# Expert slots of 448, 384 and 256 tokens for the experts' rests, in a fused retention, expert and feed-forward kernel

## Chip, cores and metric

One core of one Trainium2 chip. The metric is the device time of one execution, in microseconds (us); lower is better. Three runs of the kernel before have a median of 1375.33 us.

## What is computed

Three steps over 4608 tokens of 512 features, all in float32 (cut from the reference):

```python
# 1. retention: 8 batches, 8 heads, 576 positions, 64 features a head
ret = scale * (q @ k.T) * Dmat           # Dmat: causal, gamma_h ** (i - j)
x = (ret @ v) as (4608, 512)
# 2. experts: each token goes to one of 8
logits = x @ w_gate + modality_bias[modality_id]
e_idx = argmax(logits, axis=1)
gate_w = softmax(logits)[e_idx]
for e in range(8):
    mask = e_idx == e
    h = maximum(x[mask] @ w1[e], 0.0)    # 512 -> 1024
    out[mask] = gate_w[mask] * (h @ w2[e])   # 1024 -> 512
# 3. feed-forward
h = maximum(out @ w_in, 0.0)             # 512 -> 2048
return (h * h) @ w_out                   # 2048 -> 512
```

How many tokens an expert gets is known only when the kernel has computed the logits.

## The kernel before

**Stages.** `phase0` computes the retention and the routing, tile by tile of 128 tokens. `phase12` runs the experts. `phase3` runs the feed-forward, with an order of instructions that a planner (`Plan`) makes from a list of costs; the change doesn't touch it. The order of the other two is written out by hand.

**Slots.** Tokens of one expert are gathered into a slot and computed together. There are ten slots: `"E"`, of 512 tokens, takes the first 512 of the expert that leads after 32 of the 36 tiles, so that work can begin before the routing is done; slots 0 to 7 are 512 wide and slot 8 (`NF`) is 256 wide. Behind them stand seven guarded slots (`extra`, `NX`), which run only if the count `slots[:, 3]` says so: one branch, passed by all engines at unit 73, skips them together. A guarded slot goes over its weights twice, for two output columns at a time, with one buffer of each kind.

**Units.** A slot is eight units (`us`, index i), one for each 128 of the 1024 inner features. In unit i TensorE runs `first` of unit i+1 (12 matmuls: 4 blocks of 128 features, each in three terms of high and low parts) and then `second` of unit i (12 more, into four banks). The moving operand is as wide as the slot (`width`). ScalarE makes `hh` (the rectified product), VectorE `hl` (what is left over). Transposes of the next slot (`trans`, four of them per 128 features, one for each 128 tokens) stand between the two halves of units 3 to 6; ScalarE and VectorE split them into `xh` and `xl`. First products and transposes rotate through three banks.

**Beside it**, in the same hand-written order: weight loads (`wload`, three buffers `wr`), their split (`wsplit`, `wx` and `wy`, one per unit, four units ahead), the conversion of the float64 weights of the last stage (`convs`, dealt out at 2250 of its cost units per unit), and `combos`, which reads 512 finished columns (`eyr`) and makes the seven operands of the first block of `phase3`. SyncE issues nearly all transfers, in order; GpSimd issues the gathers (`gather`: a register load from `slots`, a copy of indices `ix`, one indirect transfer for each 128 tokens).

**The table.** `table` computes on VectorE, in 128 equal rows, what each slot holds: `slots[:, 0]` the expert, `slots[:, 1]` the first block in the token list, `slots[:, 2]` the output column at which it starts, `slots[:, 3]` the number of guarded slots. It is a generator: ten of its steps are taken in unit 1, between the steps of the last `route_b`; ten in unit 2; the rest in unit 3. Before, an expert's tokens fill consecutive slots, rounded up, and the expert whose last slot is emptiest comes last; if there are nine slots and that last piece is 256 or smaller, it goes into slot 8.

Of the kernel before, what the change touches and what calls it, by code (L numbers as in the profile page):

```python
# [9 lines left out]
F32 = mybir.dt.float32  # L10
# [15 lines left out]
P = 128  # L26
NTILE = NT // P
TS = 512
NF = 8
NX = 7  # L30
NS = NF + 1 + NX
KD = DM // P
LC = P + NE
DMAX = NTILE
# [10 lines left out]
def consts():  # L45
    gamma = 1.0 - 2.0 ** (-5.0 - np.arange(H, dtype=np.float64))
    scale = 1.0 / np.sqrt(float(D))
    tok = np.arange(9 * P)
    pos = (tok % S).astype(np.float64)
    vdec = scale * gamma[None, :] ** (-(pos[:, None] + 1.0))  # L50
    vdec = vdec.reshape(9, P, H).transpose(1, 0, 2)
    p = np.arange(S, dtype=np.float64)
    od = gamma[:, None] ** (p[None, :] + 1.0)
    od = od.reshape(KD, 2, 1, S)
    od[1::2] = od[1::2, ::-1].copy()
    odec = np.repeat(od, D, axis=2)
# [11 lines left out]
    rows["k512"] = 512.0 * np.arange(9)  # L68
    e = np.arange(NE)
    rows["le"] = (e[None, :] <= e[:, None]).astype(np.float64).reshape(-1)  # L70
    rows["eid"] = e
    rows["e36"] = DMAX * e
    s = np.arange(NS)
    rows["sv"] = np.where(s <= NF, s, s - 1)
# [17 lines left out]
def kernel(ctx, tc, qT, kT, kN, vN, modT, w_gate, mbias, w1, w2, w_in, w_out,  # L92
# [209 lines left out]
    def table():  # L302
        ps = count(NTILE, "psc")
        yield
        st = s1.tile([P, 4, NE], F32, tag="st", name="st")
        cm = s1.tile([P, NE, 9], F32, tag="cm", name="cm")
        rm = s1.tile([P, NE], F32, tag="rem", name="rem")
        mn = s1.tile([P, 1], F32, tag="mn", name="mn")
        isl = s1.tile([P, NE], F32, tag="isl", name="isl")
        nl = s1.tile([P, NE], F32, tag="nl", name="nl")  # L310
        le = s1.tile([P, NE, NE], F32, tag="le", name="le")
        en = s1.tile([P, NE], F32, tag="en", name="en")
        sn = s1.tile([P, NE], F32, tag="sn", name="sn")
        tot = s1.tile([P, 1], F32, tag="tot", name="tot")
        rl = s1.tile([P, 1], F32, tag="rl", name="rl")
        et = s1.tile([P, 1], F32, tag="et", name="et")
        mm = s1.tile([P, 2, NS, NE], F32, tag="mm", name="mm")
        ww = s1.tile([P, 4, NS, NE], F32, tag="ww", name="ww")
        rr = s1.tile([P, 4, NS], F32, tag="rr", name="rr")
        kk = s1.tile([P, NS], F32, tag="kk", name="kk")  # L320
        nsl, cnt = st[:, 0, :], st[:, 1, :]
        sv = row("sv")
        dve.scalar_tensor_tensor(out=cnt, in0=ise, scalar=-float(TS), in1=ps, op0=ALU.mult, op1=ALU.add)
        dve.tensor_copy(st[:, 2, :], row("eid"))
        dve.scalar_tensor_tensor(out=st[:, 3, :], in0=ise, scalar=4.0, in1=row("e36"), op0=ALU.mult,
                                 op1=ALU.add)
        yield
        dve.tensor_tensor(out=cm, in0=bc(cnt.unsqueeze(2), [P, NE, 9]),
                          in1=bc(row("k512").unsqueeze(1), [P, NE, 9]), op=ALU.is_gt)
        yield  # L330
        dve.tensor_reduce(out=nsl, in_=cm, axis=AX.X, op=ALU.add)
        yield
        dve.scalar_tensor_tensor(out=rm, in0=nsl, scalar=-float(TS), in1=cnt, op0=ALU.mult, op1=ALU.add)
        yield
        dve.tensor_reduce(out=mn, in_=rm, axis=AX.X, op=ALU.min)
        yield
        for _ in first_max(rm, mn, ALU.is_le, isl, "l"):
            yield
        dve.tensor_scalar(out=nl, in0=isl, scalar1=-1.0, scalar2=1.0, op0=ALU.mult, op1=ALU.add)
        yield  # L340
        dve.tensor_tensor(out=le, in0=row("le").rearrange("p (a b) -> p a b", a=NE),
                          in1=bc(nl.unsqueeze(1), [P, NE, NE]), op=ALU.mult)
        yield
        dve.tensor_tensor(out=le, in0=le, in1=bc(isl.unsqueeze(2), [P, NE, NE]), op=ALU.max)
        yield
        dve.tensor_tensor(out=le, in0=le, in1=bc(nsl.unsqueeze(1), [P, NE, NE]), op=ALU.mult)
        yield
        dve.tensor_reduce(out=en, in_=le, axis=AX.X, op=ALU.add)
        yield
        dve.tensor_tensor(out=sn, in0=en, in1=nsl, op=ALU.subtract)  # L350
        dve.tensor_tensor(out=mm[:, 0], in0=bc(en.unsqueeze(1), [P, NS, NE]),
                          in1=bc(sv.unsqueeze(2), [P, NS, NE]), op=ALU.is_le)
        dve.tensor_reduce(out=tot, in_=en, axis=AX.X, op=ALU.max)
        yield
        dve.tensor_tensor(out=mm[:, 1], in0=bc(sn.unsqueeze(1), [P, NS, NE]),
                          in1=bc(sv.unsqueeze(2), [P, NS, NE]), op=ALU.is_le)
        dve.tensor_tensor(out=ww[:, 0:2], in0=bc(mm[:, 0:1], [P, 2, NS, NE]),
                          in1=bc(st[:, 0:2, :].unsqueeze(2), [P, 2, NS, NE]), op=ALU.mult)
        dve.tensor_scalar(out=rl, in0=mn, scalar1=-256.0, scalar2=None, op0=ALU.is_le)
        yield  # L360
        dve.tensor_tensor(out=mm[:, 1], in0=mm[:, 1], in1=mm[:, 0], op=ALU.subtract)
        dve.scalar_tensor_tensor(out=rl, in0=tot, scalar=float(NF + 1), in1=rl, op0=ALU.is_equal,
                                 op1=ALU.mult)
        yield
        dve.tensor_tensor(out=ww[:, 2:4], in0=bc(mm[:, 1:2], [P, 2, NS, NE]),
                          in1=bc(st[:, 2:4, :].unsqueeze(2), [P, 2, NS, NE]), op=ALU.mult)
        yield
        dve.tensor_reduce(out=rr, in_=ww, axis=AX.X, op=ALU.add)
        yield
        dve.tensor_tensor(out=kk, in0=sv, in1=rr[:, 0, :], op=ALU.subtract)  # L370
        dve.tensor_copy(slots[:, 0, :], rr[:, 2, :])
        dve.tensor_scalar(out=tot, in0=tot, scalar1=-float(NF), scalar2=0.0, op0=ALU.add, op1=ALU.max)
        yield
        dve.tensor_scalar(out=kk, in0=kk, scalar1=8.0, scalar2=None, op0=ALU.min)
        dve.tensor_scalar(out=et, in0=rl, scalar1=-1.0, scalar2=1.0, op0=ALU.mult, op1=ALU.add)
        yield
        dve.scalar_tensor_tensor(out=slots[:, 1, :], in0=kk, scalar=4.0, in1=rr[:, 3, :], op0=ALU.mult,
                                 op1=ALU.add)
        dve.scalar_tensor_tensor(out=kk, in0=kk, scalar=float(TS), in1=rr[:, 1, :], op0=ALU.mult,
                                 op1=ALU.add)  # L380
        dve.tensor_tensor(out=tot, in0=tot, in1=et, op=ALU.mult)
        yield
        dve.tensor_scalar(out=kk, in0=kk, scalar1=float(TS), scalar2=float(NT), op0=ALU.add, op1=ALU.min)
        dve.tensor_scalar(out=et, in0=et, scalar1=float(NT), scalar2=None, op0=ALU.mult)
        dve.tensor_copy(slots[:, 3, :], bc(tot[:, 0:1], [P, NS]))
        yield
        dve.tensor_tensor(out=kk[:, NF:NF + 1], in0=kk[:, NF:NF + 1], in1=et, op=ALU.max)
        yield
        dve.tensor_copy(slots[:, 2, :], kk)
        yield  # L390

    def run(gen, n):
        for _ in range(n):
# [45 lines left out]
    X, XG = {}, {}  # L439

    def width(s):
        return 256 if s == NF else TS

    def gather(s):
        nt = width(s) // P
        rmax = (NTILE - G) * P if s == "E" else NT
        src = eslot[0:1, 1:2] if s == "E" else slots[0:1, 1, s:s + 1]
        reg = pool.value_load(src, min_val=0, max_val=KEYS - nt)
# [242 lines left out]
    def phase12():  # L691
        ring[0] = psG
        with ExitStack() as c1:
# [63 lines left out]
            def trans(s, c):  # L757
# [80 lines left out]
            def second(u, cols=range(KD)):  # L838
# [9 lines left out]
                if f == 7:  # L848
# [16 lines left out]
                    sp.dma_start(so.rearrange("(j p) -> j p", p=P), td[bass.ds(key, nt), :])  # L865

# [112 lines left out]
            for i, u in enumerate(us):  # L979
# [422 lines left out]
```

## Time and profile before

| | us |
|---|---|
| median of three runs | 1375.33 |
| lowest and highest | 1374.15, 1376.38 |
| the profiled execution | 1375.41 |
| its span, first to last instruction | 1373.6 |
| TensorE busy | 1334.8 |
| VectorE busy | 1022.4 |
| ScalarE busy | 627.4 |

The profile was taken in one execution; PE is TensorE, PEld its weight loads, DVE VectorE, ACT ScalarE, POOL GpSimd and SP SyncE. A matmul's recorded length includes its way through the array, so records overlap: the distance between starts is what one costs. "Idle before" is the time in which an engine stood still ahead of an instruction, with what ended it.

### The profile page before, as it was taken

To read this page: it belongs to the slowest core of one execution; us is meant where nothing else is said; L and a number is where in the kernel's file an instruction comes from. 1 tells how busy PE (TensorE), PEld (TensorE's weight loads), DVE (VectorE), ACT (ScalarE), POOL (GpSimd) and SP (SyncE) were. 2 spreads that over 40 slices of the span, in tenths; PEclk is the share of its full clock that TensorE was granted. 3 is DMA by queue.
4 is the path that set the end of the run, shared out by engine and by line. 5 is a ranking of instruction groups with operands and counts; after the bars stand their busy time and mean duration, and the time that the engine had idled before them with its cause. 6 is when DMAs were issued, how large, how long until landed. Compare 5 with 4: busy or idle time off the path is not lost.

```text
span 1373.6 us, 26947 instructions
## 1 busy us (share of the span) xinstructions
PE 1334.8 (97%) x10643; PEld 1228.3 (89%) x10643; DVE 1022.4 (74%) x2077; ACT 627.4 (46%) x1283; POOL 131.0 (10%) x170
## 2 busy tenths in 40 slices
PE   6999999999999999999999999999999999999997
PEld 5888877888888888879999999999999999999997
DVE  2787857878787787554888888867887777776765
ACT  1444444454445445444655555543344344443333
POOL 3222114101110110000000000000000011111121
PEclk9999999999999999999999999999999999999999
DMA  9988256778786886669545554577799756564451
GB/s 332 386 303 295 91 195 231 272 278 283 246 288 236 302 277 216 240 232 342 226 187 207 211 212 185 207 269 270 288 337 339 279 229 209 200 213 170 169 183 48
DMA packets 139380, 332.55 MB, mean 242 GB/s; under 512 B 15568, under 2 KB 50160, under 8 KB 139248
## 3 DMA queue, kind: packets, MB, share of 16 engines
q1 hardware_dynamic: 131120, 310.21, 63.1%
q0 software_dynamic: 5920, 19.40, 4.0%
q8 instruction: 84, 1.38, 0.4%
q10 hardware_dynamic: 2208, 1.17, 0.3%
q14 instruction: 48, 0.39, 0.1%
HBM read 222.59 MB, written 108.17 MB: 241 GB/s over the span
## 4 chain that ended last, share of the span: by engine, by line
PE 47%; DMA 3%; DVE 2%; ACT 0%; issue 0%; POOL 0%; SPq 0%; POOLq 0%
PE bank L1176 16%; PE bank L1174 16%; PE bank L1175 16%; DMA w<-wc 3%; DVE z L1152 1%; DVE h L1277 0%; DVE z L1160 0%; ACT h L1276 0%; POOL out L1284 0%; SPq L1047 0%; DVE oe L1152 0%; ACT z L1149 0%; DVE x L1152 0%; DVE yr L1152 0%; POOLq L1398 0%
## 5 line engine op out<-in xcount | busy, mean ns | idle before, releaser
L1174 PE MATMUL bank<-x,w 128*128 128x256 f32 x1008 | 285.9, 284 | 1.2 <-ACT z L1149 1.1
L1175 PE MATMUL bank<-w,h 128*128 128x256 f32 x1008 | 282.8, 281 | 3.7 <-DMA w<-wc 3.7
L1175 PE MATMUL bank<-x,w 128*128 128x256 f32 x1008 | 285.8, 284 | 0.5 <-DVE x L1152 0.5
L1174 PE MATMUL bank<-w,h 128*128 128x256 f32 x1008 | 282.7, 280 | 2.9 <-DVE oe L1152 1.6
L1176 PE MATMUL bank<-x,w 128*128 128x256 f32 x1008 | 285.0, 283 | 0.0
L1176 PE MATMUL bank<-w,h 128*128 128x256 f32 x1008 | 282.2, 280 | 0.7 <-DVE h L1277 0.7
L1149 ACT ACTIVATE z<-bank 128x256 f32<-128x256 f32 x288 | 108.7, 380 | 255.5 <-PE bank L1176 253.5
L1174 PEld LDWEIGHTS bank<-x,w 128*128 128x128 f32 x1008 | 192.6, 191 | 2.7 <-ACT z L1149 2.7
L1276 ACT ACTIVATE h<-z 128x512 fp32r<-128x512 f32 (+2 forms) x270 | 158.2, 598 | 80.0 <-DVE z L1152 63.7
L1175 PEld LDWEIGHTS bank<-x,w 128*128 128x128 f32 x1008 | 192.9, 191 | 1.1 <-DVE x L1152 0.7
L1174 PEld LDWEIGHTS bank<-w,h 128*128 128x128 f32 x1008 | 190.0, 189 | 4.0 <-DVE oe L1152 2.2
L1175 PEld LDWEIGHTS bank<-w,h 128*128 128x128 f32 x1008 | 189.6, 188 | 4.4 <-DMA w<-wc 4.3
L1176 PEld LDWEIGHTS bank<-x,w 128*128 128x128 f32 x1008 | 193.1, 192 | 0.0
L1176 PEld LDWEIGHTS bank<-w,h 128*128 128x128 f32 x1008 | 189.7, 188 | 0.9 <-DVE h L1277 0.9
L1277 DVE TENSOR_TENSOR h<-z,h 128x512 fp32r<-128x512 f32 (+2 forms) x270 | 168.7, 648 | 7.8 <-ACT h L1276 7.8
L1152 DVE TENSOR_TENSOR z<-z,bank 128x256 f32<-128x256 f32 x216 | 89.2, 416 | 68.8 <-PE bank L1176 50.0
L815 PE MATMUL bank<-hh,wy 128*128 128x512 f32 (+1 forms) x320 | 125.3, 392 | 0.0
L815 PE MATMUL bank<-xh,wx 128*128 128x512 f32 (+1 forms) x320 | 122.9, 384 | 1.7 <-DVEq L934 1.7
L816 PE MATMUL bank<-xl,wx 128*128 128x512 f32 (+1 forms) x320 | 122.7, 383 | 1.1 <-DVE xl L771 1.1
L817 PE MATMUL bank<-xh,wx 128*128 128x512 f32 (+1 forms) x320 | 123.5, 386 | 0.0
L817 PE MATMUL bank<-hh,wy 128*128 128x512 f32 (+1 forms) x320 | 123.3, 385 | 0.0
L816 PE MATMUL bank<-hl,wy 128*128 128x512 f32 (+1 forms) x320 | 122.6, 383 | 0.0
(172 smaller groups left out, 2135.9 us busy)
## 6 DMA issues: line engine op xcount, KB each, us to landing
x<-xc SPq DMA_DIRECT2D x112, 512.0 KB
wr<-w SPq DMA_DIRECT2D x80, 512.0 KB
xc<-x SPq DMA_DIRECT2D x63, 512.0 KB
w<-wc SPq DMA_DIRECT2D x32, 896.0 KB
wc<-cwh SPq DMA_DIRECT2D x16, 896.0 KB
wc<-cwl SPq DMA_DIRECT2D x16, 896.0 KB
pd<-oe SPq DMA_DIRECT2D x24, 512.0 KB
xd<-xs SPq DMA_DIRECT2D x9, 1024.0 KB
```

Of the source, the lines that this page charges most:

```text
L815: pe.matmul(ps, lh, rh, start=first, stop=False)
L816: pe.matmul(ps, lh, rl, start=False, stop=False)
L817: pe.matmul(ps, ll, rh, start=False, stop=last)
L1149: plan.add(a_(c), lambda e: e.activation(o, i, f), r, w)
L1152: plan.add(engs or d_(c), lambda e: e.tensor_tensor(out=o, in0=a, in1=b, op=op), r, w)
L1174: e.matmul(ps[n], lh, rh, start=first and n == 0, stop=False, skip_group_check=True)
L1175: e.matmul(ps[n], lh, rl, start=False, stop=False, skip_group_check=True)
L1176: e.matmul(ps[n], ll, rh, start=False, stop=True, skip_group_check=True)
L1276: plan.add(a_(c), lambda e: e.activation(h[:, 0, a:b], z[:, a + 1:b + 1], AF.Copy), rs, ks[0])
L1277: plan.add(d_(c), lambda e: e.tensor_tensor(out=h[:, 1, a:b], in0=z[:, a + 1:b + 1], in1=h[:, 0, a:b].bitcast(F32), op=ALU.subtract), rs + ...
```

## The change

The rests of the experts, what is left after full slots of 512, get slots of their own. All full pieces of all experts come first, in slots from 0 on; then the rests, sorted by size, the largest first. Slot 6 is 448 wide, slot 7 is 384 and slot 8 is 256. A comparison finds whether the piece in slot 6 fits, then whether those in 7 and 8 do as well; from the first that doesn't fit, the pieces are done in guarded slots (`base` is the first guarded piece), and the others' output goes to spare columns. There are nine guarded slots instead of seven. The table is made in two parts: the nine fixed slots and the guards' count (up to `"set"`, in unit 3), then the guarded slots' entries (in unit 4, behind `tab_turn`). `combos` is taken in units 65 (one step) and 66 to 69 (two steps each), instead of 68 on with three steps each. The diff, with the table cut to its frame:

```diff
-NX = 7
+NX = 9
 NS = NF + 1 + NX
+WIDE = {NF - 2: 448, NF - 1: 384, NF: 256}
...
+        dve.tensor_reduce(out=full, in_=cm, axis=AX.X, op=ALU.add)
+        yield
+        dve.scalar_tensor_tensor(out=rem, in0=full, scalar=-float(TS), in1=cnt, op0=ALU.mult, op1=ALU.add)
...
+        for x in range(2):
+            dst = slots[:, :, NX * x:NX * x + NX]
...
+            dve.tensor_tensor(out=ww, in0=bc(mm[:, 0].rearrange("p n a e -> p n (a e)").unsqueeze(1),
+                                             [P, 4, NX, 2 * NE]),
+                              in1=bc(vv.rearrange("p c a e -> p c (a e)").unsqueeze(2), [P, 4, NX, 2 * NE]),
+                              op=ALU.mult)
+            yield
+            dve.tensor_reduce(out=rr, in_=ww, axis=AX.X, op=ALU.add)
+            yield
+            dve.tensor_copy(dst[:, 0], rr[:, 0, :])
...
+            dve.tensor_scalar(out=dst[:, 1], in0=rr[:, 1, :], scalar1=float(KEYS - 4), scalar2=None, op0=ALU.min)
...
+            if x:
+                dve.tensor_copy(dst[:, 2], rr[:, 2, :])
+                yield
+                return
+            dve.tensor_tensor(out=fit, in0=rr[:, 3, NF - 2:], in1=row("wid"), op=ALU.is_le)
...
+            dve.tensor_scalar(out=slots[:, 3, 0:1], in0=tot, scalar1=0.0, scalar2=None, op0=ALU.max)
+            yield
+            dve.tensor_scalar(out=sx, in0=row("sv"), scalar1=base[:, 0:1], scalar2=None, op0=ALU.add)
+            sv = sx
+            yield "set"
...
     def width(s):
-        return 256 if s == NF else TS
+        return WIDE.get(s, TS)
+
+    def blocks(s):
+        return -(-width(s) // P)
 
     def gather(s):
-        nt = width(s) // P
+        nt = blocks(s)
...
-                for j in range(wd // P):
+                for j in range(blocks(s)):
                     pe.transpose(ps[:, j, :], xg[:, j, c * P:c * P + P], ident)
...
-                    nt = wd // P
+                    nt = blocks(s)
...
-                        yo, so = yd[:, bass.ds(reg, wd)], sd[bass.ds(reg, wd)]
+                        yo, so = yd[:, bass.ds(reg, wd)], sd[bass.ds(reg, nt * P)]
...
                 elif i == 3:
-                    for _ in tb:
+                    while next(tb) != "set":
                         pass
+                    turn = chain(turn, tb)
                     ws(8, 2, 11)
                 else:
                     wl(i + 9)
                     run(turn, 9)
                     fill(wsg(i + 6, 2 if i < 10 else 1, i + 9), part(cs, 2250))
-                    if i >= 68:
-                        run(ex, 3)
+                    if i >= 65:
+                        run(ex, 1 if i == 65 else 2)
```

## Rows read from the trace of the kernel before

**Rows 1.** The page's busy times: us (share of the span) and instructions, by engine.

```profile
PE 1334.8 (97%) x10643; PEld 1228.3 (89%) x10643; DVE 1022.4 (74%) x2077; ACT 627.4 (46%) x1283; POOL 131.0 (10%) x170
```

**Rows 2.** Windows: stretch, length, busy us by engine, clock, DMA share, GB/s.

```profile
510.00:557.00 47.00, 47.00 (x212) 37.96 (x211) 37.56 (x46) 22.48 (x32) 1.91 (x2) 1.00 0.74 261
557.00:604.87 47.87, 47.56 (x209) 38.00 (x208) 22.93 (x32) 19.48 (x30) 0.00 (x0) 1.00 0.53 184
604.87:634.06 29.19, 26.47 (x207) 25.47 (x205) 13.44 (x21) 12.15 (x24) 0.00 (x0) 1.00 0.87 323
```

**Rows 3.** Timeline of PE: start us, length, instruction, count, idle before; around the first gather.

```profile
228.58 0.77 PE L768 MATMUL bank<-ident,xg 128*128 128x128 f32 x5 [2.67 <-DMA xg<-xd,ix]
...
232.79 0.48 PE L815 MATMUL bank<-xh,wx 128*128 128x512 f32 x1
```

**Rows 4.** Waits of PE over the span: us in total, times, longest.

```profile
PE bank L815 <- DVEq L934: 1.7, 1, 1.7
...
PE bank L816 <- DVE xl L771: 1.1, 1, 1.1
```

**Rows 5.** Waits of PE from 540 to 700 us.

```profile
PE bank L1175 <- DMA w<-wc: 2.0, 2, 1.3
```

**Rows 6.** Groups by line and form: count, busy us, mean ns, idle before.

```profile
L815 PE MATMUL bank<-hh,wy 128*128 128x512 f32 x288 | 116.3, 404 | 0.0
...
L815 PE MATMUL bank<-hh,wy 128*128 128x256 f32 x32 | 9.1, 283 | 0.0
```

**Rows 7.** Timeline of PE, width 512: first and last of 23 matmuls in a row.

```profile
199.58 0.39 PE L816 MATMUL bank<-xl,wx 128*128 128x512 f32 x1
...
204.71 0.40 PE L817 MATMUL bank<-hh,wy 128*128 128x512 f32 x1
```

**Rows 8.** Timeline of PE, width 256: first and last of 35 matmuls in a row.

```profile
618.34 0.28 PE L816 MATMUL bank<-xl,wx 128*128 128x256 f32 x1
...
622.42 0.28 PE L817 MATMUL bank<-xh,wx 128*128 128x256 f32 x1
```

**Rows 9.** Timeline of PE: four transposes and the matmul after them.

```profile
508.98 0.60 PE L768 MATMUL bank<-ident,xg 128*128 128x128 f32 x4
509.33 0.48 PE L815 MATMUL bank<-hh,wy 128*128 128x512 f32 x1
```

**Rows 10.** GpSimd: register loads (ns min/median/max, first and last start), and a gather's issue.

```profile
L448 POOLq TENSOR_LOAD <-slots x9: 285/297/987, 211.4 to 499.0; - x9
...
218.24 4.39 POOL L453 DMA_INDIRECT xg<-xd,ix  x1 [0.30 <-issue]
```

**Rows 11.** Timeline in unit 2 and 3: a weight split, and its reader on PE.

```profile
204.05 1.22 DVE L156 TENSOR_TENSOR wx<-wr,wx 128x1024 fp32r<-128x1024 f32 x1
...
205.94 0.40 PE L817 MATMUL bank<-xh,wx 128*128 128x512 f32 x1
```

**Rows 12.** Timeline of DVE: the table's two widest operations.

```profile
209.09 0.43 DVE L365 TENSOR_TENSOR ww<-mm,st 128x256 f32<-128x256 f32 x1
209.55 0.69 DVE L368 TENSOR_REDUCE rr<-ww 128x64 f32<-128x512 f32 x1
```

**Rows 13.** Timeline of DVE in units 4 to 6.

```profile
221.82 0.69 DVE L728 TENSOR_SCALAR cwk<-cwk 128x1024 int32<-128x1024 int32 x1
...
223.69 0.68 DVE L832 SCALAR_TENSOR_TENSOR hl<-bank,hh 128x512 fp32r<-128x512 f32 x1
...
227.97 0.68 DVE L832 SCALAR_TENSOR_TENSOR hl<-bank,hh 128x512 fp32r<-128x512 f32 x1
```

**Rows 14.** Timeline of DVE: the first operation of `combos`.

```profile
599.29 0.69 DVE L785 TENSOR_TENSOR etx<-eyr 128x512 f32<-128x512 f32 x1 [6.15 <-DMA eyr<-yd]
```

**Rows 15.** Timeline of SP's queue: start us, length of the issues, what is loaded, count.

```profile
593.59 0.51 SPq L778 DMA_DIRECT2D eyr<-yd  x1
...
615.39 1.12 SPq L419 DMA_DIRECT2D wr<-w  x1
...
622.63 4.36 SPq L1047 DMA_DIRECT2D w<-wc  x8
```

More of the change, by code (lines that the diff above doesn't have):

```diff
@@ L67, in consts @@
     rows["rev"] = 8.0 - np.arange(NE)
-    rows["k512"] = 512.0 * np.arange(9)
+    rows["k512"] = 512.0 * np.arange(1, 9)
     e = np.arange(NE)
-    rows["le"] = (e[None, :] <= e[:, None]).astype(np.float64).reshape(-1)
+    rows["lt"] = (e[None, :] < e[:, None]).astype(np.float64).reshape(-1)
     rows["eid"] = e
     rows["e36"] = DMAX * e
-    s = np.arange(NS)
-    rows["sv"] = np.where(s <= NF, s, s - 1)
+    rows["sv"] = np.arange(NF + 1)
+    rows["wid"] = np.array([WIDE[s] for s in range(NF - 2, NF + 1)])
     off, cat, o = {}, [], 0
@@ L304, in table @@
         yield
[L305 to L311, printed above, removed]
+        cnt = s1.tile([P, NE], F32, tag="cnt", name="cnt")
+        cm = s1.tile([P, NE, 8], F32, tag="cm", name="cm")
@@ L312, in table @@
+        full = s1.tile([P, NE], F32, tag="full", name="full")
+        rk = s1.tile([P, NE], F32, tag="rk8", name="rk8")
+        t3 = s1.tile([P, 3, NE, NE], F32, tag="t3", name="t3")
+        r3 = s1.tile([P, 3, NE], F32, tag="r3", name="r3")
         en = s1.tile([P, NE], F32, tag="en", name="en")
-        sn = s1.tile([P, NE], F32, tag="sn", name="sn")
+        pi = s1.tile([P, NE], F32, tag="pi", name="pi")
+        nf = s1.tile([P, 1], F32, tag="nf", name="nf")
         tot = s1.tile([P, 1], F32, tag="tot", name="tot")
-        rl = s1.tile([P, 1], F32, tag="rl", name="rl")
@@ L316, in table @@
[L316 to L322, printed above, removed]
-        dve.scalar_tensor_tensor(out=cnt, in0=ise, scalar=-float(TS), in1=ps, op0=ALU.mult, op1=ALU.add)
-        dve.tensor_copy(st[:, 2, :], row("eid"))
@@ L325, in table @@
-        dve.scalar_tensor_tensor(out=st[:, 3, :], in0=ise, scalar=4.0, in1=row("e36"), op0=ALU.mult,
+        base = s1.tile([P, 1], F32, tag="base", name="base")
+        fit = s1.tile([P, 3], F32, tag="fit", name="fit")
+        vv = s1.tile([P, 4, 2, NE], F32, tag="vv", name="vv")
+        mm = s1.tile([P, 2, NX, 2, NE], F32, tag="mm", name="mm")
+        ww = s1.tile([P, 4, NX, 2 * NE], F32, tag="ww", name="ww")
+        rr = s1.tile([P, 4, NX], F32, tag="rr", name="rr")
+        sx = s1.tile([P, NX], F32, tag="sx", name="sx")
@@ new lines, in table @@
+        rank, left, sn = (r3[:, k, :] for k in range(3))
+        rem, kb = vv[:, 3, 1, :], vv[:, 1, 0, :]
+        dve.scalar_tensor_tensor(out=cnt, in0=ise, scalar=-float(TS), in1=ps, op0=ALU.mult, op1=ALU.add)
+        dve.tensor_copy(vv[:, 0], bc(row("eid").unsqueeze(1), [P, 2, NE]))
+        dve.scalar_tensor_tensor(out=kb, in0=ise, scalar=4.0, in1=row("e36"), op0=ALU.mult, op1=ALU.add)
+        yield
+        dve.tensor_tensor(out=cm, in0=bc(cnt.unsqueeze(2), [P, NE, 8]),
+                          in1=bc(row("k512").unsqueeze(1), [P, NE, 8]), op=ALU.is_ge)
@@ new lines, in table @@
+        dve.memset(vv[:, 2, 0, :], 0.0)
+        dve.memset(vv[:, 3, 0, :], float(TS))
+        yield
+        dve.tensor_reduce(out=full, in_=cm, axis=AX.X, op=ALU.add)
+        yield
+        dve.scalar_tensor_tensor(out=rem, in0=full, scalar=-float(TS), in1=cnt, op0=ALU.mult, op1=ALU.add)
+        dve.tensor_reduce(out=nf, in_=full, axis=AX.X, op=ALU.add)
+        yield
+        dve.scalar_tensor_tensor(out=rk, in0=rem, scalar=8.0, in1=row("rev"), op0=ALU.mult, op1=ALU.add)
+        dve.tensor_tensor(out=t3[:, 2], in0=row("lt").rearrange("p (a b) -> p a b", a=NE),
+                          in1=bc(full.unsqueeze(1), [P, NE, NE]), op=ALU.mult)
@@ new lines, in table @@
+        yield
+        dve.tensor_tensor(out=t3[:, 0], in0=bc(rk.unsqueeze(1), [P, NE, NE]),
+                          in1=bc(rk.unsqueeze(2), [P, NE, NE]), op=ALU.is_gt)
+        dve.scalar_tensor_tensor(out=vv[:, 1, 1, :], in0=full, scalar=4.0, in1=kb, op0=ALU.mult, op1=ALU.add)
+        yield
+        dve.tensor_tensor(out=t3[:, 1], in0=t3[:, 0], in1=bc(rem.unsqueeze(1), [P, NE, NE]), op=ALU.mult)
+        yield
+        dve.tensor_reduce(out=r3, in_=t3, axis=AX.X, op=ALU.add)
+        yield
@@ new lines, in table @@
+        dve.tensor_scalar(out=pi, in0=rank, scalar1=nf[:, 0:1], scalar2=None, op0=ALU.add)
+        dve.tensor_tensor(out=en, in0=sn, in1=full, op=ALU.add)
+        yield
+        dve.scalar_tensor_tensor(out=vv[:, 2, 1, :], in0=rank, scalar=-float(TS), in1=left, op0=ALU.mult,
+                                 op1=ALU.add)
+        dve.scalar_tensor_tensor(out=kb, in0=sn, scalar=-4.0, in1=kb, op0=ALU.mult, op1=ALU.add)
+        dve.scalar_tensor_tensor(out=vv[:, 1, 1, :], in0=pi, scalar=-4.0, in1=vv[:, 1, 1, :], op0=ALU.mult,
@@ L326, in table @@
                                  op1=ALU.add)
         yield
[L328 to L335, printed above, removed]
@@ L336, in table @@
-        yield
-        for _ in first_max(rm, mn, ALU.is_le, isl, "l"):
-            yield
[L339 to L389, printed above, removed]
@@ L390, in table @@
-        yield
+        sv = row("sv")
+        for x in range(2):
+            dst = slots[:, :, NX * x:NX * x + NX]
+            m = bc(sv.unsqueeze(2), [P, NX, NE])
+            dve.tensor_tensor(out=mm[:, 0, :, 0, :], in0=bc(sn.unsqueeze(1), [P, NX, NE]), in1=m, op=ALU.is_le)
+            dve.tensor_tensor(out=mm[:, 1, :, 0, :], in0=bc(en.unsqueeze(1), [P, NX, NE]), in1=m, op=ALU.is_gt)
+            dve.tensor_tensor(out=mm[:, 0, :, 1, :], in0=bc(pi.unsqueeze(1), [P, NX, NE]), in1=m, op=ALU.is_equal)
+            yield
+            dve.tensor_tensor(out=mm[:, 0, :, 0, :], in0=mm[:, 0, :, 0, :], in1=mm[:, 1, :, 0, :], op=ALU.mult)
+            yield
+            dve.tensor_tensor(out=ww, in0=bc(mm[:, 0].rearrange("p n a e -> p n (a e)").unsqueeze(1),
+                                             [P, 4, NX, 2 * NE]),
+                              in1=bc(vv.rearrange("p c a e -> p c (a e)").unsqueeze(2), [P, 4, NX, 2 * NE]),
+                              op=ALU.mult)
+            yield
+            dve.tensor_reduce(out=rr, in_=ww, axis=AX.X, op=ALU.add)
+            yield
+            dve.tensor_copy(dst[:, 0], rr[:, 0, :])
+            dve.scalar_tensor_tensor(out=rr[:, 1, :], in0=sv, scalar=4.0, in1=rr[:, 1, :], op0=ALU.mult, op1=ALU.add)
+            dve.scalar_tensor_tensor(out=rr[:, 2, :], in0=sv, scalar=float(TS), in1=rr[:, 2, :], op0=ALU.mult,
+                                     op1=ALU.add)
+            yield
+            dve.tensor_scalar(out=dst[:, 1], in0=rr[:, 1, :], scalar1=float(KEYS - 4), scalar2=None, op0=ALU.min)
+            dve.tensor_scalar(out=rr[:, 2, :], in0=rr[:, 2, :], scalar1=float(TS), scalar2=float(NT), op0=ALU.add,
+                              op1=ALU.min)
+            if x:
+                dve.tensor_copy(dst[:, 2], rr[:, 2, :])
+                yield
+                return
+            dve.tensor_tensor(out=fit, in0=rr[:, 3, NF - 2:], in1=row("wid"), op=ALU.is_le)
+            yield
+            dve.tensor_tensor(out=fit[:, 1:2], in0=fit[:, 0:1], in1=fit[:, 1:2], op=ALU.mult)
+            dve.tensor_scalar(out=cm[:, 0, :], in0=rem, scalar1=0.0, scalar2=None, op0=ALU.is_gt)
+            yield
+            dve.tensor_tensor(out=fit[:, 2:3], in0=fit[:, 1:2], in1=fit[:, 2:3], op=ALU.mult)
+            dve.tensor_reduce(out=tot, in_=cm[:, 0, :], axis=AX.X, op=ALU.add)
+            yield
+            dve.tensor_reduce(out=base, in_=fit, axis=AX.X, op=ALU.add)
+            yield
+            dve.tensor_scalar(out=base, in0=base, scalar1=float(NF - 2), scalar2=None, op0=ALU.add)
+            dve.tensor_tensor(out=tot, in0=tot, in1=nf, op=ALU.add)
+            yield
+            dve.tensor_scalar(out=sx, in0=sv, scalar1=base[:, 0:1], scalar2=float(NT), op0=ALU.is_ge, op1=ALU.mult)
+            dve.tensor_tensor(out=tot, in0=tot, in1=base, op=ALU.subtract)
+            yield
+            dve.tensor_tensor(out=dst[:, 2], in0=rr[:, 2, :], in1=sx, op=ALU.max)
+            dve.tensor_scalar(out=slots[:, 3, 0:1], in0=tot, scalar1=0.0, scalar2=None, op0=ALU.max)
+            yield
+            dve.tensor_scalar(out=sx, in0=row("sv"), scalar1=base[:, 0:1], scalar2=None, op0=ALU.add)
+            sv = sx
+            yield "set"
```

## The prediction, made before the kernel ran

> **What bounds the kernel now.** I read the page's busy times first, then the stage windows, then the waits of TensorE, then the timelines of the three places that the change touches. TensorE is busy for 97% of the span [rows 1]. While the experts run, its busy time equals the stretch: 47.00 of 47.00 us in the slot that starts at 510 us, 47.56 of 47.87 us in the next; the granted clock is 1.00, the 2.4 GHz level, and VectorE is the nearest other engine with 37.56 of 47 us [rows 2]. So the experts' stage costs what its matmuls cost, and fewer columns shorten it at once. Around the stage TensorE waits little: 2.67 us for the gather of the first slot [rows 3], 1.1 us for a transposed slice and 1.7 us at the guard [rows 4], 2.0 us for the weights of the last stage [rows 5].
>
> **Do the rests fit?** I counted the routing that the reference's inputs give: 1949, 2289 and 370 tokens go to three experts, none to the other five. The early slot takes 512 of one of the two large ones. Whichever it is, six full slots and rests of 413, 370 and 241 are left. Before, the 413 and the 370 sit in slots of 512 and the 241 in the 256 slot. After, they sit in 448, 384 and 256, with 35, 14 and 15 places free; nine slots hold all nine pieces. So no guarded slot runs, in either kernel.
>
> **Matmuls: -16.3 us.** Each slot has 192 of them (eight units of 24): the 1728 at width 512 and the 192 at width 256 are six groups of each width; one of either stands in [rows 6]. Durations of single matmuls overlap, so I take start-to-start times. Width 512: from 199.58 to 204.71 us are 22 steps, 0.2332 us each [rows 7]. Width 256: from 618.34 to 622.42 us are 34 steps, 0.1200 us each [rows 8]. Widths 448 and 384 are not in this trace. The bounds are the two neighbours: as dear as 512 (gain 0) or as cheap as 256 (192 x 2 x 0.1132 = 43.5 us). Between them I take the straight line, 0.1132/256 = 0.442 ns per column, because a column costs nearly the same in both rows (0.455 and 0.469 ns). That gives 0.2049 and 0.1766 us: 192 x 0.0283 = 5.4 us for the 448 slot, 192 x 0.0566 = 10.9 us for the 384 slot. All of it is on TensorE's own path.
>
> The Trainium skill (TensorE: Matmul & The Clock Gate, "Back-to-back issue gap") gives the isolated gap as columns / 2.4 ns plus 2.5 ns, so the skill's saving would be 192 x 192 / 2.4 = 15.4 us, and the sum 0.9 us longer. The rows are 17 and 11 ns above it; by them the line stands.
>
> **Transposes: -0.3 us.** The 384 slot has three blocks, so four of its transposes go. Four in a row take 0.35 us until the next matmul starts [rows 9], 0.09 each. Its fourth gather goes too; that queue is not on the path.
>
> **The table: 0.** It is computed on VectorE by hand between the units of the early slot, in 10 + 10 + rest steps. The new one puts some eight more small operations into the first ten (about 0.1 us each, by their spacing), the same amount into the next, and ends with five instead of eight. What waits: GpSimd's register load for the first gather, which starts at 211.4 us [rows 10], right after the write of the start blocks, not at the table's end. That write now stands in the second ten. I estimate it some 0.85 us earlier: +0.85 (first ten), then 2.7 us of work where 4.2 us stood. SyncE's load of the expert number is equally early. First cost: the weight split for unit 4 ends 205.27 us, the matmul that reads it starts at 205.94 us [rows 11]; 0.85 us later it holds TensorE by some 0.3 us. Second: twelve operations for the guarded slots follow the table's transposition in the next unit, two of them on 576 elements. The rows with 256 and 512 elements are 0.43 and 0.69 us [rows 12]; I get 2.7 us in all. Behind them wait the weight splits, four conversion operations, and then `hl` of units 6 and 7, at 223.69 and 227.97 us [rows 13].
>
> What comes of the 2.67 us wait? The fourth issue of the first gather starts at 218.24 us and lasts 4.39 us [rows 10], to the end of a conversion operation on VectorE at 222.5 us [rows 13]. Started 0.85 us earlier and with those 2.7 us later, it should be short, and the transposes at 228.58 [rows 3] come in time. But then `hl` of unit 7 is late: about 230.7 instead of 227.97 us, and the two `xl` after it end about 232.5. The banks that they free are those of the next transposes and of the first slot's first product, which starts at 232.79 now [rows 3]. So VectorE takes the place of the gather. I count 0 for the whole front; the bounds are -2.7 (wait gone, nothing in its place) and +1.2 us (0.3, plus 0.9 for a chain that is all late).
>
> The Trainium skill (SBUF — State Buffer, "Who interferes with whom") says that VectorE's two-port operations lock GpSimd out of a shared pair of ports for their whole length. The 4.39 us agree, ending 0.1 us after such an operation; by this rule, too, the fourth issue becomes short. It alone would make the front -2.7 us.
>
> **The `combos` steps: -0.9 us.** They moved from units 68 to 71, three steps at a time, to units 65 to 69, one and then two. Now VectorE stands 6.15 us behind the load of `eyr` [rows 14], because the load and its first uses are in one unit; TensorE pays 1.1 us there [rows 4] and 0.3 us more. After, a unit lies between the two, but it is only 24 x 0.177 = 4.24 us, and the load takes 599.29 - 593.59 = 5.7 us [rows 14, 15]. Queued behind VectorE's wait is `hl` of the next unit, and ScalarE's copy for the same step stands ahead of `hh`. Normally `hl` has one half unit, 2.1 us, and more in hand. I take 0.5 us of stalls for today's 1.4. Bounds: -1.4, and +4 (the whole 5.7 us, less the slack, shows up).
>
> **Weights of the last stage: -1.0 us.** SyncE issues eight loads of `w` at 622.63 us, seven after the last expert load at 615.39 [rows 15], for which it stands at the guard; the `combos` stores had filled the queue. With the stores done earlier, the same loads start sooner against TensorE, and of 2.0 us waiting [rows 5] half should go; bounds -2.0 and 0.
>
> **Does the rest still hide?** Conversion work is dealt out by units. In the 448 slot a unit is 24 x 0.205 plus transposes, 5.1 us; VectorE's share is 37.56/8 = 4.7 us [rows 2], 4.5 with narrower `hl` and `xl`: 88%. In the 384 slot `hl` 0.5, `xl` 0.2, split 1.2 and two `combos` steps 1.9 make 3.8 of 4.24 us. The transfers of the last two slots, 47.87 x 184 + 29.19 x 323 GB/s = 18.2 MB [rows 2], now have 61 us: 298 GB/s, under the 323 seen. Nothing becomes the bound by its mean; the margins of 10% are thin.
>
> **Sum.** -16.3 - 0.3 + 0 - 0.9 - 1.0 = -18.5 us. The profiled execution took 1375.41 us (its span 1373.6 us), 0.08 us from the median, so it needs no correction: 1356.9 us.
>
> **The rivals.**
> - *A shortened slot finds another bound.* VectorE or the transfers, at nearly 90%, lag in bursts, and `hl` comes late in the two slots. For it: the thin margins, the `eyr` wait. Against it: today's stalls from the same cause are 1.4 us. It would give back 4 to 8 us: 1361 to 1365.
> - *The front gap closes as well* and the last stage's weights come in time: -16.6 - 2.7 - 1.4 - 2.0: 1352.7. Against it speaks the `hl` chain above.
> - *The columns don't buy time*: matmuls of 448 and 384 run at the 512 pace. Then only the small terms are left, about 1373. Against it: 256 columns run at little over half.
> - *Guarded slots run* (the slower side). It decides as soon as the sorted rests exceed 448, 384 or 256; with a misfit in the first, all three rests are done again. Price of one: 288 matmuls of 0.2332 us = 67 us, as the first product is done twice, and eight pairs of weight loads, none ahead, at about 5.7 us [rows 14, 15] and 3.5 us of splits (1.2 us is one on VectorE [rows 11], and as much is ScalarE's): 73 us. So about 140 us each, 1497 with one. Against it: the count above; the smallest margin is 14 tokens.
>
> **Chances.** Forecast 0.65, another bound 0.14, front closed 0.14, columns for nothing 0.04, guarded slots 0.03. A change under 0.2%, 2.8 us, can't be told from none here. Faster: 0.93; within 0.2%: 0.04; slower: 0.03. The range takes in the closed front and most of the second bound: 1352.5 to 1363.
>
> **What would show it.** Right: matmuls 128x448 and 128x384, 192 of each, stepping 0.205 and 0.177 us; no second entry at the guard; the first slot's first product near 232.8 us; `w` loads closer behind TensorE's guard. Wrong: steps of 0.233 us; waits of the two slots on `hl`, or on banks; a wait for `eyr` that reaches TensorE; a guard that is taken.

## The result, and the profile after

The changed kernel takes 1351.77 us (median of 5 executions, 1350.09 to 1351.99) against 1375.33: ratio 0.9832, interval 0.9819 to 0.9844. That is 23.6 us less, where 18.5 were forecast, and 0.7 us under the low end of the range. The direction was right, and narrower matmuls did pay; but something worth 6.6 us in the six slots that stay 512 wide, and more in the others, was not in the sum at all.

The page's span and busy times of the changed kernel, to set beside [rows 1]:

```profile
span 1349.9 us, 26957 instructions
...
PE 1311.7 (97%) x10639; PEld 1224.7 (91%) x10639; DVE 1022.7 (76%) x2095; ACT 624.3 (46%) x1283; POOL 125.2 (9%) x169
```

TensorE lost 23.1 us of busy time for four matmuls (the transposes) fewer; VectorE has 18 instructions more and 0.3 us more to do. So nearly all of the gain is matmul time, not waiting. Where? I cut the span at the first products: of the early slot, of slots 0, 6, 7 and 8, and of the last stage. Windows of the changed kernel, columns as in [rows 2]:

```profile
184.62:232.16 47.54, 45.10 (x210) 36.05 (x208) 39.89 (x117) 19.83 (x29) 9.57 (x11) 1.00 0.68 222
232.16:505.05 272.89, 272.89 (x1249) 225.69 (x1249) 224.98 (x278) 136.22 (x186) 28.36 (x29) 1.00 0.79 272
505.05:546.20 41.15, 40.97 (x205) 37.00 (x204) 32.95 (x43) 21.03 (x30) 2.53 (x2) 1.00 0.75 258
546.20:584.20 38.00, 35.22 (x201) 34.20 (x200) 27.11 (x41) 20.18 (x33) 0.00 (x0) 1.00 0.81 287
584.20:610.92 26.72, 25.36 (x206) 25.15 (x205) 9.02 (x13) 9.72 (x19) 0.00 (x0) 1.00 0.89 343
610.92:1349.90 738.98, 724.30 (x6050) 719.20 (x6048) 567.38 (x1209) 349.13 (x768) 39.07 (x72) 1.00 0.61 223
```

The same cuts in the kernel before lie at 184.81, 232.79, 512.23, 558.79, 604.99 and 634.06 us; its slots 0 to 5:

```profile
232.79:512.23 279.44, 279.44 (x1251) 225.79 (x1250) 225.46 (x278) 136.92 (x186) 29.55 (x30) 1.00 0.78 267
```

In us:

| stretch | before | after | difference |
|---|---|---|---|
| up to the early slot | 184.81 | 184.62 | -0.2 |
| early slot | 47.98 | 47.54 | -0.4 |
| slots 0 to 5, all 512 wide in both | 279.44 | 272.89 | **-6.6** |
| slot 6 | 46.56 | 41.15 | -5.4 |
| slot 7 | 46.20 | 38.00 | -8.2 |
| slot 8 | 29.07 | 26.72 | -2.4 |
| last stage | 739.54 | 738.98 | -0.6 |

The third line is the surprise: six slots with the same matmuls, the same granted clock (1.00) and no wait of TensorE in either kernel, and still 6.6 us less. Single matmuls there, 61 in a row in the second of those slots (start us, length):

```profile
277.79 0.39 PE L838 MATMUL bank<-xh,wx 128*128 128x512 f32 x1
...
291.39 0.39 PE L838 MATMUL bank<-hh,wy 128*128 128x512 f32 x1
```

A step is the distance between the starts of two neighbouring matmuls. 13.60 us for 60 steps: 0.2267 us each, where [rows 7] had 0.2332 over 22 steps (0.2333 over 60 in the same place as here). The narrow widths, 23 in a row at 448 and 25 at 384:

```profile
513.06 0.36 PE L840 MATMUL bank<-hh,wy 128*128 128x448 f32 x1
...
517.51 0.37 PE L838 MATMUL bank<-hh,wy 128*128 128x448 f32 x1
...
551.82 0.33 PE L839 MATMUL bank<-xl,wx 128*128 128x384 f32 x1
...
555.98 0.34 PE L839 MATMUL bank<-xl,wx 128*128 128x384 f32 x1
```

4.45/22 = 0.2023 us and 4.16/24 = 0.1733 us, a little under the 0.2049 and 0.1766 of the line.

TensorE's waits from 500 to 700 us in the changed kernel, to set beside [rows 4, 5]:

```profile
PE bank L791 <- DVE hl L855: 2.7, 1, 2.7
PE bank L838 <- DVEq L957: 1.4, 1, 1.4
```

The wait at the guard stays (1.7 became 1.4), that for the weights of the last stage is gone from this window, and a transpose now waits 2.7 us for `hl`.

### The profile page after: what moved, and what is told of

The parts are those of the page before. It is cut to its first block, busy times and chain, and to the rows that moved or that the text cites. A ratio compares the mean times of both kernels' runs of the same rounds, so it can differ in the third digit from the quotient of the medians.

```text
span 1349.9 us, 26957 instructions
## 1 busy us (share of the span) xinstructions
PE 1311.7 (97%) x10639; PEld 1224.7 (91%) x10639; DVE 1022.7 (76%) x2095; ACT 624.3 (46%) x1283; POOL 125.2 (9%) x169
## 4 chain that ended last, share of the span: by engine, by line
PE 50%; DVE 4%; ACT 1%; issue 0%; POOL 0%; POOLq 0%; DVEq 0%
PE bank L1200 17%; PE bank L1198 16%; PE bank L1199 16%; DVE z L1176 2%; DVE h L1301 1%; DVE z L1184 1%; ACT h L1300 0%; PE bank L838 0%; PE bank L840 0%; PE bank L839 0%; POOL out L1308 0%; DVE oe L1176 0%; ACT z L1173 0%; DVE x L1176 0%; DVE yr L1176 0%
## 5 line engine op out<-in xcount | busy, mean ns | idle before, releaser
L838 PE MATMUL bank<-hh,wy 128*128 128x512 f32 (+3 forms) x320 | 121.9, 381 | 0.0
L838 PE MATMUL bank<-xh,wx 128*128 128x512 f32 (+3 forms) x320 | 119.2, 372 | 1.4 <-DVEq L957 1.4
L839 PE MATMUL bank<-hl,wy 128*128 128x512 f32 (+3 forms) x320 | 119.0, 372 | 0.2 <-DVE hl L855 0.2
L839 PE MATMUL bank<-xl,wx 128*128 128x512 f32 (+3 forms) x320 | 118.9, 372 | 0.1
L840 PE MATMUL bank<-xh,wx 128*128 128x512 f32 (+3 forms) x320 | 119.0, 372 | 0.0
L840 PE MATMUL bank<-hh,wy 128*128 128x512 f32 (+3 forms) x320 | 118.9, 371 | 0.0
```

The costliest lines, as they stand in the source:

```text
L838: pe.matmul(ps, lh, rh, start=first, stop=False)
L839: pe.matmul(ps, lh, rl, start=False, stop=False)
L840: pe.matmul(ps, ll, rh, start=False, stop=last)
```

## The experiments

In the profiled executions of the kernels below the last stage takes from 738.4 to 741.2 us, though the change and the experiments leave its instructions alone. The experiments ran in three groups, on different chips, each beside the kernel before, whose median was 1373.47 us in the first group (both shifts by 32 bytes, the wide slots, `combos` in unit 64), 1374.15 in the second (shifts by 160, 64 and 128 bytes, everything by 32) and 1376.41 in the third (shift by 192, `hh` and `hl` alone, the late table, all three together). Ratios are to the kernel before of the same group. So beside times I read stage lengths, cut as above.

### Does the place of the operands set the step?

What differs between two kernels whose 512 wide matmuls are the same? The new table needs 928 bytes more per partition, so everything allocated behind it moved. In the program's address list (it comes from building the program, not from the trace) the moving operands `xh`, `xl`, `hh`, `hl` started 224 bytes past a multiple of 256 before, and start 128 past one now; the weights `wx`, `wy` are 128 past one in both. My first theory was the start address alone (before, it was 32 bytes off a multiple of 64); the rival was that other work had slowed the step. The edit puts unused bytes ahead of the four tiles:

```diff
+            c1.enter_context(tc.tile_pool(name="pad", bufs=1)).tile([P, 8], F32, name="gap0")
             xp = c1.enter_context(tc.tile_pool(name="xp", bufs=2))
```

The kernel before, moved to a multiple of 256:

> The kernel before, with 32 unused bytes per partition ahead of xh, xl, hh and hl, so that these moving operands start at multiples of 64 bytes (they stood 32 bytes past one). Theory address: the start address sets the step of the 512 wide matmuls; it falls from 0.2333 to 0.2267 us, 1728 of them save 9 to 11 us: 1364 to 1366 us. Rival traffic: the step was slower because of what else ran at the time (transfers, other engines); then it stays at 0.2333 and the time at 1375 within 2 us.

Measured: 1374.17 us, ratio 1.0006 (0.999 to 1.0022).

```profile
279.67 0.40 PE L816 MATMUL bank<-xh,wx 128*128 128x512 f32 x1
...
293.67 0.40 PE L816 MATMUL bank<-hh,wy 128*128 128x512 f32 x1
```

60 steps in 14.00 us: 0.2333. The address theory in this form missed. But the other direction did move:

> The changed kernel, with the same 32 bytes, so that the moving operands start 32 bytes past a multiple of 64, as in the kernel before. Theory address: the 512 step rises to 0.2333 us (1344 of them, 8 to 9 us), 448 and 384 to the 0.205 and 0.177 us of the prediction's line (about 1.5 us more): 1360 to 1362 us, which leaves the prediction's own terms about right. Rival traffic: 1352 us and 0.2267 us.

Measured: 1360.11 us, ratio 0.9909 (0.9882 to 0.9935).

```profile
279.29 0.39 PE L839 MATMUL bank<-xh,wx 128*128 128x512 f32 x1
...
293.29 0.39 PE L839 MATMUL bank<-hh,wy 128*128 128x512 f32 x1
```

0.2333 again, from 32 unused bytes; slots 0 to 5 take 279.03 us. Slot 6 stays at 41.17 and slot 7 at 37.86 us: the slots of 448 and 384 don't get longer, against that part of the expectation. So place does count, but a multiple of 64 isn't the rule. What the kernel before with 32 bytes and the changed kernel don't share is the place of the moving operand against the weights: 128 bytes apart in the one (mod 256), 0 in the other. From here on, distance means how far the moving operand's start lies behind the weights', modulo 256 bytes. Four more kernels test that. The kernel before with `[P, 40]` (160 bytes), which makes it 0:

> The kernel before with 160 unused bytes ahead of xh, xl, hh and hl: they start 128 bytes past a multiple of 256, as in the changed kernel, and as the weights wx and wy do. (A shift by 32, to a multiple of 256, had left the 512 step at 0.233 us.) Theory low address bits: the place within 256 bytes, by itself or against the weights, sets the step: 0.2267 us, 1364 to 1366 us. Rival: it is not the low address bits but something else that the change brought: 0.2333 us and 1374 us.

Measured: 1367.55 us, ratio 0.9955 (0.9937 to 0.9972).

```profile
279.35 0.39 PE L816 MATMUL bank<-xh,wx 128*128 128x512 f32 x1
...
292.95 0.39 PE L816 MATMUL bank<-hh,wy 128*128 128x512 f32 x1
```

13.60 us, 0.2267: the step of the changed kernel, in the kernel before, by an address alone. Slots 0 to 5 take 272.83 us. The whole falls by 6.6 us against that group's kernel before and not to the 1364 to 1366 us expected; in the profiled execution the early slot is longer, 49.70 us against 47.98, with more waiting for the first gather.

```profile
PE bank L769 <- DMA xg<-xd,ix: 3.6, 2, 2.4
```

The changed kernel with 64 and with 128 bytes:

> The changed kernel with 64 unused bytes ahead of the moving operands: 192 past a multiple of 256, a multiple of 64 still. If any multiple of 64 did, 0.2267 us and 1351 us. If the place within 256 bytes counts, 0.2333 us and 1359 to 1361 us.

> The changed kernel with 128 unused bytes: the moving operands start at multiples of 256, the weights 128 past one. If a multiple of 128 does: 0.2267 us, 1351 us. If the place must be that of the weights within 256 bytes: 0.2333 us, 1359 to 1361 us, as the kernel before with 32 bytes showed.

Measured, one execution each: 1350.86 us with 64 and 1357.75 with 128; 13.73 us for 60 steps with 64, in between:

```profile
277.66 0.39 PE L839 MATMUL bank<-xh,wx 128*128 128x512 f32 x1
...
291.39 0.39 PE L839 MATMUL bank<-hh,wy 128*128 128x512 f32 x1
```

That is 0.2288 us; with 128 it is 14.00 us again, 0.2333. Neither expectation for 64 had a step in between. Is it the distance or the place itself? Weights and moving operands are moved together by 32 bytes:

```diff
+    ctx.enter_context(tc.tile_pool(name="pad", bufs=1)).tile([P, 8], F32, name="gap0")
     wp = ctx.enter_context(tc.tile_pool(name="wp", bufs=10))
```

> The changed kernel with 32 unused bytes ahead of the weights' pool too: wx, wy and the moving operands are all 32 bytes further, their distance stays. Theory distance: 0.2267 us in the experts. Theory absolute place: 0.2333 us, about 8 us slower. In the last stage some moving operands and weights change their distance as well; there the 256 step of 0.120 us may rise or not.

Measured, one execution: 1348.71 us.

```profile
275.69 0.39 PE L839 MATMUL bank<-xh,wx 128*128 128x512 f32 x1
...
289.29 0.39 PE L839 MATMUL bank<-hh,wy 128*128 128x512 f32 x1
```

0.2267 at a place (160 past a multiple of 256) that was slow when the weights stood elsewhere. So the place by itself doesn't decide; a distance does. That the weights are the other end of it is argued, not shown: every tile allocated from the weights' pool on moved with them. For the weights speaks that 60 steps in a row take 13.60 us in three different kernels, whatever other engines do meanwhile, and that each of these matmuls has a weight load of its own. The last stage, some of whose operands changed distance, took 738.56 us, as ever. Two more kernels test the other side of the distance and, in turn, `hh` and `hl` alone 32 bytes off (the pad stands ahead of the pool `hp` then):

> The changed kernel with 192 unused bytes ahead of the moving operands: they start 192 bytes (mod 256) behind the weights. Seen so far: distance 0 gives 0.2267 us, 64 gives 0.229, 32, 96 and 128 give 0.233. Theory distance, even on both sides: as 64, 0.229 us, slots 0 to 5 in 274 to 275 us. If only the way forward counts, 0.2333 us and 279 us.

> The changed kernel with 32 unused bytes ahead of hh and hl alone; xh and xl stay 0 bytes (mod 256) from the weights. Theory distance, operand by operand: the second products step at 0.2333 us, the first at 0.2267, slots 0 to 5 take 276 us, half way. If one operand alone decides, 279 or 273 us.

Measured, one execution each: with 192 the step is 0.2333 and slots 0 to 5 take 279.62 us: it isn't even on both sides, which missed. With `hh` and `hl` alone they take 277.47 us, between 272.89 and 279.03 but beyond half way. The times, 1361.71 and 1359.66 us, hold a long last stage (741.2 and 740.9 us) each. Three starts of that kernel, 12 matmuls apart, show why it is beyond half way:

```profile
281.62 0.40 PE L839 MATMUL bank<-hh,wy 128*128 128x512 f32 x1
...
284.42 0.40 PE L839 MATMUL bank<-xh,wx 128*128 128x512 f32 x1
...
287.18 0.40 PE L839 MATMUL bank<-hh,wy 128*128 128x512 f32 x1
```

The second products step at 0.2333 us, as expected; the first at 0.2300, not 0.2267, though their own distance is 0: the first six of these twelve at 0.2322, the last six at 0.2273. So it isn't operand by operand alone: the slow step reaches some way into the next half.

| distance of moving operand behind weights, mod 256 bytes | step at 512, us | slots 0 to 5, us | kernels |
|---|---|---|---|
| 0 | 0.2267 | 272.8 to 272.9 | changed; before + 160; all + 32 |
| 32 | 0.2333 | 279.0 | changed + 32 |
| 64 | 0.2288 | 274.4 | changed + 64 |
| 96 | 0.2333 | 279.4 | before |
| 128 | 0.2333 | 279.2, 279.3 | before + 32; changed + 128 |
| 192 | 0.2333 | 279.6 | changed + 192 |

This order holds for width 512 only. In slot 8, 256 wide, the same 60 steps are, in the changed kernel and then with 64 bytes:

```profile
600.84 0.28 PE L838 MATMUL bank<-xh,wx 128*128 128x256 f32 x1
...
608.04 0.28 PE L838 MATMUL bank<-hh,wy 128*128 128x256 f32 x1
```

```profile
600.65 0.28 PE L839 MATMUL bank<-xh,wx 128*128 128x256 f32 x1
...
607.45 0.28 PE L839 MATMUL bank<-hh,wy 128*128 128x256 f32 x1
```

7.20 us at distance 0 (0.1200 each) and 6.80 at 64 (0.1133). In the other traces these 60 take 7.20 us at 96, 7.12 at 128, 7.00 at 32 and 6.80 at 192. So at 256 wide the distance 0 is among the slowest, by 6%, and slot 8 falls from 26.72 to 25.77 us with 64 bytes; at 448 wide 36 steps take 7.29 us at 0 and 7.20 at 64.

### What are the narrower slots worth by themselves?

```diff
-WIDE = {NF - 2: 448, NF - 1: 384, NF: 256}
+WIDE = {NF - 2: 512, NF - 1: 512, NF: 256}
```

> The changed kernel with slots 6 and 7 at 512 again (WIDE 512, 512, 256); order, table, combos and addresses stay. Theory columns: 192 x (64 + 128) columns come back at one column per 0.417 ns, 15.4 us, and four transposes 0.3, less a shorter wait for eyr in longer units (1 to 2 us): 1365 to 1367 us. Rival: the new table and the moved combos gave part of the gain; then the columns are worth less and it ends under 1362 us.

Measured: 1363.18 us, ratio 0.9916 (0.9896 to 0.9935), between the two expectations: with no slot narrower than before, the kernel is still some 10 us faster than the kernel before beside it. Its span is 1361.7 us, 11.8 more than the changed kernel's. Slots 6, 7 and 8 take 45.46, 44.52 and 27.40 us here, against 41.15, 38.00 and 26.72: 11.5 us. It has no wait for `hl` in these slots; the changed kernel has one of 2.7 us and one of 0.2. With these set aside the widths bring 14.4 us, close to 192 x (0.0244 + 0.0534) = 14.9 from the steps. The wait was larger than thought. So the narrower slots, with the waits that come with them, are worth about half of the 23.6 us.

### Where does the new wait for `hl` come from?

```diff
-                    if i >= 65:
-                        run(ex, 1 if i == 65 else 2)
+                    if i == 64 or i >= 66:
+                        run(ex, 1 if i == 64 else 2)
```

> The changed kernel with the first step of combos (the load of eyr) in unit 64 instead of 65, none in 65, two in each of 66 to 69. Theory: VectorE waited 6.0 us behind that load and TensorE 2.7 us behind hl; a unit more of 4.2 us ahead takes the 2.7 us wait away: 1349 us. Rival: the load only queues behind the last conversion stores and lands no earlier, or another wait takes its place: 1351 to 1352 us.

Measured: 1349.63 us, ratio 0.9818 (0.98 to 0.9837). VectorE at its first use of `eyr`, in the changed kernel and then in this one:

```profile
570.41 0.69 DVE L808 TENSOR_TENSOR etx<-eyr 128x512 f32<-128x512 f32 x1 [5.99 <-DMA eyr<-yd]
```

```profile
569.25 0.69 DVE L808 TENSOR_TENSOR etx<-eyr 128x512 f32<-128x512 f32 x1 [3.93 <-DMA eyr<-yd]
```

TensorE's wait for `hl` there falls from 2.7 to 0.6 us:

```profile
PE bank L791 <- DVE hl L855: 0.6, 1, 0.6
```

and slot 7 from 38.00 to 36.07 us. SyncE issues the load, here and (further down) in the changed kernel, at:

```profile
559.15 1.30 SPq L801 DMA_DIRECT2D eyr<-yd  x1
```

Slot 7 starts at 546.98 us here and at 546.20 in the changed kernel. Counted from there the load is issued 2.4 us earlier, not a unit of 4.2, and its first use comes 1.9 us earlier, which is what slot 7 gains. So the late load made the wait: the stage shows it; in the time the 2 us are at the edge of what the intervals tell.

### Does VectorE hold the front?

```diff
-                    turn = chain(turn, tb)
...
+                    if i == 12:
+                        run(tb, 9)
```

> The changed kernel with the table's second part (the guarded slots' entries) in unit 12 instead of unit 4. Theory of the prediction: the 2.9 us that it takes on VectorE in unit 4 delay hl of units 6 and 7 and with them the first slot's first product; without it the early slot, 47.5 us from its first product to the first slot's, falls to about 45.1 us, the time to 1349 us. Rival: the gather's landing or the transposes hold it all the same: 47 us and 1351 to 1352 us.

Measured: 1353.3 us (1350.08 to 1355.53), ratio 0.9833 (0.9807 to 0.986). The early slot falls to 45.67 us as the theory said, and of TensorE's 2.4 us of waiting for `hl` there, 0.7 stay:

```profile
PE bank L791 <- DVE hl L855: 0.7, 1, 0.7
```

The time doesn't show it: in the profiled execution the last stage took 740.97 us, 2.0 more than in the changed kernel, and slot 7 38.99, 1.0 more; and the ratio is that of the changed kernel, within the intervals.

### All three together

> The changed kernel with three edits: the table's second part in unit 12, the first step of combos in unit 64, and 32 unused bytes ahead of the weights' pool (weights and moving operands keep their distance; the early slot began 2 us sooner there). If their gains add: 2.4 + 2 + 2, so 1345 us. If the early start was chance: 1347. Rival: the gains share one wait: 1349.

Measured: 1348.65 us (1347.93 to 1353.49), ratio 0.9812 (0.9789 to 0.9835). Early slot 45.58, slot 7 35.97 us: both stage gains hold, 4.0 us together. The work up to the early slot took 183.92 us, so the earlier start with everything moved by 32 bytes (182.58 us) didn't come again. The interval overlaps that of the changed kernel: the stages say that this version is better, the time alone doesn't.

## Why the prediction was wrong, point by point

**What bounds the kernel** was right: where TensorE has no wait, its stretch shortens with its matmuls.

**Do the rests fit?** held: no guarded slot ran (the guard is skipped in 1.4 us).

**Matmuls: -16.3 us, the step that failed.** It took the 512 step of the trace, 0.2332 us, as a property of the width, and changed only the two slots whose width changes. But the change also lengthens the table's tiles, and with them moves the moving operands of the experts' products: from 96 bytes behind the weights (mod 256) to 0. At that distance a 512 wide step is 0.2267 us, in all seven slots that stay 512 wide: -6.6 us in slots 0 to 5. A part that is in the diff, the new sizes of the table's tiles (`vv`, `mm` and `ww` among them), was costed at nothing. The line through 512 and 256 was bent by it too: the 512 step falls with the distance from 96 to 0 and the 256 step stays at 0.1200, so the line gave 0.2049 and 0.1766 where 0.2023 and 0.1733 were measured. By those, 192 x (0.0310 + 0.0600) = 17.5 us against 16.3. That the two are close is in part luck: 14.9 of the 17.5 are the width at one and the same distance, and 2.5 (384 x 0.0066) are the distance again. Of the formula of the Trainium skill (TensorE: Matmul & The Clock Gate, "Back-to-back issue gap"), columns / 2.4 + 2.5 ns, the slope fits for 128 columns at the fast distance (0.0534 us saved, 0.0533 by it) and less well for 64 (0.0244, 0.0267 by it); its 216 ns for 512 columns were not seen here at any distance.

**Transposes**: four fewer, as said; too small to see.

**The table: 0** was right in its parts. GpSimd's load comes earlier (209.9 instead of 211.4 us, [rows 10]), the fourth gather issue is short, and `hl` of units 6 and 7 comes at 225.93 and 230.22 us ([rows 13]; 230.7 was said for the second). Register loads, that issue, the two `hl`, and TensorE's waits:

```profile
L471 POOLq TENSOR_LOAD <-slots x9: 287/294/1059, 209.9 to 491.6; - x9
...
215.54 0.94 POOL L476 DMA_INDIRECT xg<-xd,ix  x1 [0.30 <-issue]
```

```profile
225.93 0.68 DVE L855 SCALAR_TENSOR_TENSOR hl<-bank,hh 128x512 fp32r<-128x512 f32 x1
...
230.22 0.68 DVE L855 SCALAR_TENSOR_TENSOR hl<-bank,hh 128x512 fp32r<-128x512 f32 x1
```

```profile
226.67 0.66 PE L791 MATMUL bank<-ident,xg 128*128 128x128 f32 x4 [1.55 <-DVE hl L855]
...
230.96 1.25 PE L791 MATMUL bank<-ident,xg 128*128 128x128 f32 x8 [0.88 <-DVE hl L855]
232.16 0.50 PE L838 MATMUL bank<-xh,wx 128*128 128x512 f32 x1
```

The gather's 2.67 us are gone ([rows 3]), 2.43 us of waiting for `hl` stand in their place, and the first product starts at 232.16 instead of 232.79 us, though 192 matmuls ahead of it step 0.0066 us faster (1.3 us). Without that the front would have cost a little, inside the bounds. Moving the second part of the table shows it: 45.67 us. So VectorE did take the gather's place.

**The `combos` steps: -0.9 us** had the wrong sign. 1.4 us of waiting became 2.7 (and 0.2 in slot 6). The wait for `eyr` is 5.99 us, as long as before ([rows 14]): the unit in between was used up by a load that took longer. SyncE's issue, in the changed kernel:

```profile
560.78 0.52 SPq L801 DMA_DIRECT2D eyr<-yd  x1
```

From 560.78 to 570.41 are 9.6 us where 5.7 had been counted. I took the load's time from a stretch that moved 184 GB/s [rows 2]; here the stretch moves 287. That the traffic makes the load longer is argued, not shown by itself: in the 6.3 us ahead of it SyncE issues two weight loads in both kernels, and in the changed one two stores of converted weights (`wc`, 896 KB each) as well. The wait stayed inside the bound of +4.

**Weights of the last stage: -1.0 us**: the 2.0 us of [rows 5] went from TensorE's waits in that window, the stage is 0.6 us shorter, within what it varies by. Its worth is not shown either way.

**The rivals.** None of them came true as a whole: of another bound there is a part, the 2.7 us wait for `hl` in slot 7 where the rival had 4 to 8 in both slots (slot 6 has one of 0.2 us); the columns do buy time, and the guarded slots don't run. The time lies below even the rival with the front closed, 1352.7 us, with the front not closed: the moved operands, which brought it there, were in no rival.

**The sum with what was measured**: slots 6 to 8 -16.0 (widths and both waits), slots 0 to 5 -6.6, early slot -0.4, the rest -0.8: -23.7, which is the difference of the spans.

## What to carry to other kernels

A step that the trace shows, here 0.2333 us at 512 wide, is that of this program with its addresses; before it goes into a sum as a constant, ask whether the diff changes the size of any tile allocated ahead of the operands. Where a stage without waits differs between two kernels by a fixed amount per instruction, list the operands' addresses first and test with a few unused bytes: it costs one line and separates the placement from the change. Test each width that matters: what was fastest at 512 was among the slowest at 256. The last stage here has some 6000 records of matmuls 256 wide, at 0.118 to 0.121 us; at slot 8's 0.1133 that would be some 30 to 40 us, an estimate from these steps that no run tests. And time a load by the stretch that it moves into (here 9.6 us), not by that which it leaves (5.7).

## What the runs showed of the hardware

A matmul with a moving operand of 128x512 float32 steps at 0.2267 us when that operand starts at the same place within 256 bytes as the weights' tile, 0.2288 when it is 64 bytes behind, and 0.2333 at 32, 96, 128 and 192. At 256 wide the order is another: 0.1133 us at 64 and 192, 0.1167 at 32, 0.1187 at 128, 0.1200 at 0 and 96. Slots of 448 and 384 took as long at distance 32 as at 0 (41.17 and 41.15, 37.86 and 38.00 us). Moved together with all that lies behind the weights, both keep the fast step, so neither address decides by itself. The Trainium skill (TensorE: Matmul & The Clock Gate, "Step-by-step: what each phase is for") says that loading the next weights takes no read bandwidth from the running matmul; a step that depends on where the operands lie, by 2.9% at 512 wide and 6% at 256, is not what one would expect from that alone. Whether the reads of weights and moving operand meet in the memory, or something else that follows the distance does, these runs don't show; nor was it tried with other data types or with the weights alone moved.
